# Two copies of an attention stage moved from GpSimd to ScalarE, and more dummy matmuls in front of and inside it

## The chip, the cores and the metric

The kernel runs on one core of one Trainium2 chip. The metric is the device time of one execution in microseconds (us); smaller is better. A core has TensorE (PE, with its weight loads PEld), VectorE (DVE), ScalarE (ACT), GpSimd (POOL) and SyncE (SP), each with an instruction queue of its own, and DMA queues that move data between HBM and the on-chip memory (SBUF). TensorE writes to PSUM.

## What is computed

```
S = 576; gamma = 1 - 2**(-5 - head)
ret = (q @ k.T / 8) * where(i >= j, gamma**(i - j), 0)     # 4 batches, 8 heads, 576 x 64
x = ret @ v                                                # as 2304 tokens x 512
h = x @ w_in ; x = (h * sigmoid(1.702 h)) @ w_out          # 512 -> 2048 -> 512, float64 weights
e = argmax of cosine(x, expert_emb) / tau ; gate = softmax at e
out = gate * (relu(x @ w1[e]) @ w2[e])                     # 8 experts, 512 -> 1024 -> 512
```

## The kernel before

The kernel has three stages: attention (retention), a dense layer over six blocks of 384 tokens, and the experts. All times below are counted from the start of the profiled span. Attention fills the span up to 79 us, and only there does the change act.

**Attention.** A pair `bp` is two heads of one batch; there are 16 pairs, 0 to 15. One pair has four chunks of 128 positions (`ch` 0 to 3) and a tail of 64 (`ch` 4). A *step* is one (bp, ch). The order of steps is written out by hand: pairs of even and odd number take turns. It begins (0,0), (0,1), (0,2), (1,0), (0,3), (1,1), (0,4), (1,2), and from there it repeats for every pair as (b,0), (b-1,3), (b,1), (b-1,4), (b,2), so step (b,0) comes three steps ahead of (b-1,4). At step i the program issues, in this order:

- if ch is 0: `prep(bp + 2)`, the preparation of the pair after next;
- `scores(i + 2)`: eight matmuls (L275, or four at L278 for a tail) into one of three PSUM tiles, and one masking multiply on DVE (L280);
- `state(bp, ch)`: four matmuls (L302) that add to the running state in PSUM, and one scaled copy of it to SBUF on ACT (L304), tile `ends`. The next chunk of the same pair reads that copy in L318, and the next L302 may overwrite the PSUM state only when the copy has read it;
- `chunk(bp, ch)`: L318 (earlier state times queries) and L322 (masked scores times values);
- `keep`: at ch 3 and ch 4 a DVE multiply (L340, L337). For the pairs of batches 0 and 1, after ch 4 come casts on ACT (L350), a copy on ACT (L353) and subtractions on POOL (L351).

`prep(bp)` copies the two heads' queries into a zero-padded tile `qz` (two copies of 64x512, L287, POOL), multiplies the keys by decays in place (L290, POOL; DVE for pair 0), and copies the tails' queries (two copies of 64x64, L293, POOL). Pair 0's queries come by DMA. There are four `qz` tiles (NQ = 4).

A pair's data is one DMA of 1 MB (`row`, L232) into one of five buffers. Rows 1 to 4 are asked for at the start. Row bp + 5 is asked for at the end of pair bp, on SP's queue, and goes out when matmuls no longer read the buffer. The same queue carries the decay tables, the tails (L243) and, from 24.95 us on, the dense layer's weights (`wd`, L120).

**Dummies.** At the start PE runs 34 matmuls on a tile of ones (`warm`, L251); nothing reads their result.

**Beside it.** From step 37 on the conversion of the float64 weights is dealt out in small portions between attention steps: an ACT magnitude (L150), DVE integer work (L163, L165, L170, L177), an ACT cast (L153) and a DVE subtraction (L157), about two of sixteen units before attention ends.

Of the kernel before, what the change touches and what calls it, by code (L numbers as in the profile page):

```python
# [10 lines left out]
F32 = mybir.dt.float32  # L11
# [6 lines left out]
P = 128  # L18
B, H, S, HD = 4, 8, 576, 64
NPAIR = H // 2  # L20
NCH = 4
TAIL = S - NCH * P
# [14 lines left out]
ROW = D + 2  # L37
BIG = 100000.0
LAG = 2
WARM = 34  # L40
HOLD = NF1 - LAG - 1 - KD
STOP = 1000.0
WD_AT = (7, 11, 14)
# [1 line left out]
NBUF, NQ = 5, 4  # L45
# [4 lines left out]
AK, AV, AQ, AW = NCH * P, 2 * NCH * P, 3 * NCH * P, 4 * NCH * P  # L50
TQ, TV, TAW = TAIL, 2 * TAIL, 3 * TAIL
# [11 lines left out]
def retention_moe_kernel(  # L63
# [18 lines left out]
    PE, ACT, DVE, POOL, SP = nc.tensor, nc.scalar, nc.vector, nc.gpsimd, nc.sync  # L82
# [8 lines left out]
    ones = pool.tile([P, P], BF16, name="ones")  # L91
# [35 lines left out]
    def load_due():  # L127

        if st.get("loaded"):
            while due:  # L130
                load_wd(due.pop(0))
# [71 lines left out]
    def slot(name):  # L203
        st["slots"] = st.get("slots", -1) + 1
        assert st["slots"] < HELD
        return unit_tile(name, [P, 2048], F32, st["slots"])
# [6 lines left out]
    def attention_(psum):  # L213


        row = [slot(f"row{i}") for i in range(1, NBUF)]
        row.insert(0, slot("row0"))
        qz = [slot(f"qz{i}") if i > 1 else pool.tile([P, 2048], F32, tag="tab", bufs=2, name=f"qz{i}") for i in range(NQ)]
        tb = slot("tb")[:, : NPAIR * TW].rearrange("p (n w) -> p n w", w=TW)
        ends = slot("ends")  # L220
        tl = [ends[:, NPAIR * TAW * i : NPAIR * TAW * (i + 1)].rearrange("p (n w) -> p n w", w=TAW) for i in range(2)]
# [24 lines left out]
        DVE.memset(ones, 1.0)  # L246
        ACT.copy(scr, ones[:, :16])

        warm = psum.tile([P, 512], F32, tag="o", bufs=2, name="warm")
        for _ in range(WARM):  # L250
            PE.matmul(warm[:, :P], ones, ones, start=True, stop=True)  # L251
        scs = [psum.tile([P, 512], F32, name=f"sc{i}") for i in range(3)]
        for i in range(NQ):
            for j in range(2):
# [8 lines left out]
        def scores(n):  # L263
            bp, ch = steps[n]
            t, q = row[bp % NBUF], [qz[bp % NQ][:, S * j + P * ch : S * (j + 1)] for j in range(2)]
            sc = scs[n % 3][:, : 2 * P].rearrange("p (j q) -> p j q", j=2)
            pr = pool.tile([P, 2, P], F32, tag="g", bufs=6, name=f"pr{bp}_{ch}")
            st["pr", bp, ch] = pr
            w = P if ch < NCH else TAIL
            if ch < NCH:  # L270


                for j, i in ((0, 0), (0, 1), (1, 1), (1, 0)):
                    k0, q0 = P * ch + 64 * (i ^ j), 64 * (i ^ j)
                    PE.matmul(sc[64 * i : 64 * i + 64, j, q0:], t[:, k0 : k0 + 64], q[j][:, q0:P], start=True, stop=True)  # L275
            else:
                for j in range(2):
                    PE.matmul(sc[64 * j : 64 * j + 64, j, :TAIL], tl[bp // NPAIR % 2][:, bp % NPAIR, :TQ], q[j], start=True, stop=True)  # L278
            mask = tb[:, bp % NPAIR, :TD].rearrange("p (j q) -> p j q", j=2)
            DVE.tensor_tensor(pr[:, :, :w], sc[:, :, :w], mask[:, :, :w], ALU.mult)  # L280

        def prep(bp):
            t, end = row[bp % NBUF], tl[bp // NPAIR % 2][:, bp % NPAIR, TQ:TV]
            for j in range(2):
                r, q0 = slice(64 * j, 64 * j + 64), S * j
                if bp:
                    POOL.tensor_copy(qz[bp % NQ][r, q0 : q0 + NCH * P], t[r, AQ:])  # L287
            kd = t[:, AK:AV].rearrange("p (c e) -> p c e", e=HD)
            dec = tb[:, bp % NPAIR, TD + P : TD + P + 2 * NCH]
            (POOL if bp else DVE).tensor_tensor(kd, kd, dec.unsqueeze(2).to_broadcast(kd.shape), ALU.mult)  # L290
            for j in range(2):
                r, q0 = slice(64 * j, 64 * j + 64), S * j + NCH * P
                POOL.tensor_copy(qz[bp % NQ][r, q0 : q0 + TAIL], end[r])  # L293

        def state(bp, ch):
            t = row[bp % NBUF]
            if ch == 0:
                st["kv", bp] = psum.tile([P, 64], F32, tag="kv", bufs=2, name=f"s{bp}")
            s = st["kv", bp]
            for j in range(2):  # L300
                c0 = P * ch + 64 * j
                PE.matmul(s[64 * j : 64 * j + 64], t[:, AK + c0 : AK + c0 + 64], t[:, AV + c0 : AV + c0 + 64], start=ch == 0, stop=True, skip_group_check=ch > 0)  # L302
            dec = TD + P + 2 * NCH + ch
            ACT.activation(kvs[bp % 2][:, 64 * ch : 64 * ch + 64], s, AF.Copy, scale=tb[:, bp % NPAIR, dec : dec + 1])  # L304

        def chunk(bp, ch):
            t = row[bp % NBUF]
            pr = st.pop(("pr", bp, ch))
            if ch == 0:
                st["o", bp] = psum.tile([P, 512], F32, tag="o", bufs=2, name=f"ao{bp}")  # L310
            if ch == NCH:
                st["ot", bp] = psum.tile([P, 512], F32, tag="ot", bufs=1, name=f"at{bp}")
            n = P if ch < NCH else TAIL
            o = st["o", bp][:, P * ch : P * (ch + 1)] if ch < NCH else st["ot", bp][:, :TAIL]
            if ch:
                for j in range(2):
                    q0 = S * j + P * ch
                    PE.matmul(o[64 * j : 64 * j + 64], kvs[bp % 2][:, 64 * (ch - 1) : 64 * ch], qz[bp % NQ][:, q0 : q0 + n], start=True, stop=False)  # L318
            for j in range(2):
                v0 = AV + P * ch + 64 * j  # L320
                v = t[:, v0 : v0 + 64] if ch < NCH else tl[bp // NPAIR % 2][:, bp % NPAIR, TV:]
                PE.matmul(o[64 * j : 64 * j + 64], v, pr[:, j, :n], start=ch == 0, stop=True)  # L322
# [39 lines left out]
        prep(1)  # L362
        scores(0)
        scores(1)
        for i, (bp, ch) in enumerate(steps):
            if ch == 0 and bp + 2 < NBP:
                prep(bp + 2)
            if i + 2 < len(steps):
                scores(i + 2)
            if ch < NCH:  # L370
                state(bp, ch)
            chunk(bp, ch)
            if ch >= NCH - 1:
                keep(bp, ch == NCH)
            if ch == NCH:
                if bp + NBUF < NBP:
                    load(bp + NBUF)
                if bp + NBUF in WD_AT:
                    load_wd(WD_AT.index(bp + NBUF))
                if bp + NBUF + 1 == NBP:  # L380

                    st["loaded"] = True
                    SP.dma_start(c[:, :CET], cst[:, :CET])
                    SP.dma_start(c[:, CET : CET + KD * E], embt)
                    uf = pool.tile([P, P], F32, tag="cvb", bufs=1, name="uf")
                    SP.dma_start(uf, cst[:, CU:CSL])
                    load_due()
            yield
# [325 lines left out]
    psum = ctx.enter_context(tc.tile_pool(name="psum", bufs=1, space=bass.MemoryType.PSUM, reuse_waits="tile"))  # L714
# [300 lines left out]
```

## Time and profile before

| | |
|---|---|
| device time, median of 3 runs | 785.65 us (784.45 to 787.34) |
| profiled execution, its own time | 788.28 us |
| its span | 786.4 us (1.9 us lie around it) |
| PE busy | 756.7 us (96%) |
| DVE / ACT / POOL busy | 458.3 / 306.6 / 226.6 us |
| mean granted TensorE clock | 0.985 |

The profiled execution is one run; it is 2.6 us longer than the median of the unprofiled runs. [...] In rows of the timeline the first number is the start, the second the time from the first start to the last end of the merged instructions; in brackets stands the idle time before them and what ended it.

### The profile page before, as it was taken

What the parts mean: (1) busy time and instruction counts of PE and PEld (TensorE: products, weight loads), DVE (VectorE), ACT (ScalarE), POOL (GpSimd) and SP (SyncE); (2) the same over time, 40 slices, a digit from 0 to 9 for tenths busy, and PEclk for the clock granted to TensorE, in tenths of its full rate; (3) what the DMA queues carried; (4) which work ended last, traced back from release to release, by engine and by line L of the source; (5) the groups of instructions that cost most, each with busy time, mean ns of one, the idle gap of its engine ahead of it and who ended that gap; (6) DMA issues with size and microseconds to landing.
All of it is one profiled execution on the core that took longest, in us unless ns stands there. A gap on an engine that the chain in (4) does not pass through costs nothing.

```text
span 786.4 us, 13066 instructions
## 1 busy us (share of the span) xinstructions
PE 756.7 (96%) x4996; PEld 678.1 (86%) x4996; DVE 458.3 (58%) x1000; ACT 306.6 (39%) x572; POOL 226.6 (29%) x251
## 2 busy tenths in 40 slices
PE   7998999999999889999999998999999999999994
PEld 6988899999999779989989987888888888888883
DVE  4688798886368775744763886652543435444210
ACT  2453454544553232323322443434444444445221
POOL 4995000000002211210201233234544545544311
PEclk8999999999999999999999999999999999999998
DMA  9988995001200122021004234255464635545201
GB/s 346 383 339 278 400 386 199 0 1 53 108 0 1 55 68 80 1 72 51 0 1 135 81 107 132 79 178 171 157 178 131 197 134 181 180 153 176 78 31 35
DMA packets 31576, 104.95 MB, mean 133 GB/s; under 512 B 4495, under 2 KB 7439, under 8 KB 27280
## 3 DMA queue, kind: packets, MB, share of 16 engines
q1 hardware_dynamic: 27984, 93.78, 35.1%
q0 software_dynamic: 3232, 9.46, 3.3%
q8 instruction: 41, 0.67, 0.3%
q10 hardware_dynamic: 288, 0.79, 0.3%
q14 instruction: 31, 0.25, 0.1%
HBM read 80.88 MB, written 24.18 MB: 134 GB/s over the span
## 4 chain that ended last, share of the span: by engine, by line
PE 73%; DVE 10%; issue 8%; ACT 4%; DMA 3%; POOL 2%; SPq 0%; POOLq 0%; ACTq 0%; DVEq 0%
PE h L416 20%; PE o L427 20%; PE eo L427 12%; PE eh L416 12%; DVE dj L514 4%; PE sc L275 2%; PE ao L322 2%; PE ao L318 1%; DMA row<-att 1%; PE tp L619 1%; DMA we<-we 1%; PE s L302 1%; DVE unit L195 1%; POOL out L457 1%; POOL unit L196 1%
## 5 line engine op out<-in xcount | busy, mean ns | idle before, releaser
L416 PE MATMUL h<-x,unit 128*128 128x384 f32 x1152 | 219.9, 339 | 4.7 <-DVE x_k L445 2.5
L416 PEld LDWEIGHTS h<-x,unit 128*128 128x128 f32 x1152 | 205.8, 189 | 15.1 <-DVE x_k L445 3.8
L196 POOL TENSOR_TENSOR unit<-we,unit 128x512 fp32r<-128x512 f32 x64 | 105.0, 1647 | 149.7 <-ACT unit L194 149.6
L416 PE MATMUL eh<-xt,unit 128*128 128x352 f32 x672 | 117.1, 323 | 0.0
L416 PEld LDWEIGHTS eh<-xt,unit 128*128 128x128 f32 x672 | 111.0, 188 | 6.3
L514 DVE CUSTOM_DVE_ANT_0 dj<-xr,en 128x512 f32<-128x512 f32 x120 | 91.2, 813 | 0.0
L195 DVE TENSOR_TENSOR unit<-we,unit 128x512 fp32r<-128x512 f32 x64 | 58.3, 911 | 41.0 <-ACT unit L194 41.0
L194 ACT CAST unit<-we 128x1024 fp32r<-128x1024 f32 x64 | 66.8, 1046 | 7.0 <-DMA we<-we 7.0
L480 POOL TENSOR_TENSOR enrm<-scr,c 128x8 f32<-128x8 f32 x1 | 1.7, 1683 | 150.4 <-ACT ej L485 150.4
L275 PE MATMUL sc<-qz,row 128*64 128x128 f32 (+1 forms) x512 | 38.1, 252 | 5.9 <-POOL qz L287 2.4
L280 DVE TENSOR_TENSOR pr<-sc,tb 128x256 f32<-128x256 f32 (+1 forms) x80 | 30.4, 391 | 13.3 <-PE sc L275 10.3
L457 POOL DMA_INDIRECT out<-y,idx x24 | 23.6, 981 | 49.2 <-ACT y L628 47.1
L275 PEld LDWEIGHTS sc<-qz,row 128*64 128x64 f32 x512 | 29.9, 140 | 7.9 <-POOL qz L287 3.5
L304 ACT ACTIVATE ends<-s,tb 128x64 f32<-128x64 f32 x64 | 19.7, 312 | 33.0 <-PE s L302 30.5
L322 PE MATMUL ao<-pr,row 128*64 128x128 f32 x256 | 30.0, 281 | 1.1 <-DVE pr L280 1.0
L457 POOL DMA_INDIRECT xs<-xr,slot x18 | 18.7, 1040 | 35.4 <-DVE ov_all L593 23.3
L409 POOL TENSOR_TENSOR x<-x0s,x 128x768 fp32r<-128x768 f32 x3 | 6.0, 1997 | 72.6 <-ACT x L408 72.6
L302 PE MATMUL s<-row 128*64 128x64 f32 x256 | 23.3, 228 | 0.6 <-ACT ends L304 0.4
L318 PE MATMUL ao<-qz,ends 128*64 128x128 f32 x192 | 22.7, 280 | 0.0
L157 DVE TENSOR_TENSOR unit<-ca,unit 128x1024 fp32r<-128x1024 f32 x16 | 20.4, 1276 | 2.8 <-ACT unit L153 2.8
L572 POOL TENSOR_TENSOR cum<-cum,oh_all 128x8 bf16<-128x8 bf16 x18 | 3.6, 202 | 62.4 <-PE rk L565 61.5
L322 PEld LDWEIGHTS ao<-pr,row 128*64 128x64 f32 x256 | 19.6, 141 | 2.3 <-DVE pr L280 2.1
(1258 smaller groups left out, 1545.2 us busy)
## 6 DMA issues: line engine op xcount, KB each, us to landing
we<-we SPq DMA_DIRECT2D x64, 512.0 KB, 3.5
wd<-wd SPq DMA_DIRECT2D x16, 1024.0 KB, 9.9
row<-att SPq DMA_DIRECT2D x15, 1024.0 KB, 7.1
xs<-fill SPq DMA_DIRECT2D x22, 257.0 KB, 10.4
xrow<-xr SPq DMA_DIRECT2D x18, 257.0 KB, 4.8
rin<-xs SPq DMA_DIRECT2D x8, 514.0 KB, 4.6
x0d<-x0f SPq DMA_DIRECT2D x4, 768.0 KB, 10.5
x0s<-x0d SPq DMA_DIRECT2D x8, 384.0 KB, 6.4
```

Source lines behind the costliest of these rows:

```text
L194: ACT.copy(w[:, 0, :], t)
L195: DVE.tensor_tensor(w[:, 1, :512], t[:, :512], w[:, 0, :512].bitcast(F32), ALU.subtract)
L196: POOL.tensor_tensor(w[:, 1, 512:], t[:, 512:], w[:, 0, 512:].bitcast(F32), ALU.subtract)
L275: PE.matmul(sc[64 * i : 64 * i + 64, j, q0:], t[:, k0 : k0 + 64], q[j][:, q0:P], start=True, stop=True)
L280: DVE.tensor_tensor(pr[:, :, :w], sc[:, :, :w], mask[:, :, :w], ALU.mult)
L302: PE.matmul(s[64 * j : 64 * j + 64], t[:, AK + c0 : AK + c0 + 64], t[:, AV + c0 : AV + c0 + 64], start=ch == 0, stop=True, skip_group_chec ...
L318: PE.matmul(o[64 * j : 64 * j + 64], kvs[bp % 2][:, 64 * (ch - 1) : 64 * ch], qz[bp % NQ][:, q0 : q0 + n], start=True, stop=False)
L322: PE.matmul(o[64 * j : 64 * j + 64], v, pr[:, j, :n], start=ch == 0, stop=True)
L416: PE.matmul(h, w[:, a, P * dc : P * (dc + 1)], xt[:, b, dc, :n], start=k == 0, stop=k == len(terms) - 1)
L427: PE.matmul(o, a[:, c0 : c0 + n], w[:, b, 512:], start=first and k == 0, stop=last and k == 2)
L457: i = POOL.indirect_dma_start(out=dst[:, :], out_offset=bass.IndirectOffsetOnAxis(ap=rows, axis=0), in_=src, in_offset=None, bounds_check= ...
L514: DVE.tensor_tensor_reduce(junk, r[:, :D], en[e // 4][:, e % 4, :], 1.0, 0.0, ALU.mult, ALU.add, dots[:, E * k + e : E * k + e + 1])
```

## The change

Four edits, all in attention: the number of dummies in front goes from 34 to 62, and their PSUM tile from tag `o` to tag `ot`; 8 more dummies are issued after `scores(1)` and after the chunk of each of the first three steps; the second head's query copy of pairs 4 to 15 goes from POOL to ACT; the tails' query copies of all pairs go from POOL to ACT, and from `prep(bp)` (two pairs ahead) to the point behind `chunk(bp, 1)`.

```diff
-WARM = 34
+WARM = 62
...
-        warm = psum.tile([P, 512], F32, tag="o", bufs=2, name="warm")
-        for _ in range(WARM):
-            PE.matmul(warm[:, :P], ones, ones, start=True, stop=True)
+        warm = psum.tile([P, 512], F32, tag="ot", bufs=1, name="warm")
+        def run(n):
+            for _ in range(n):
+                PE.matmul(warm[:, :P], ones, ones, start=True, stop=True)
+        run(WARM)
...
         def prep(bp):
-            t, end = row[bp % NBUF], tl[bp // NPAIR % 2][:, bp % NPAIR, TQ:TV]
+            t = row[bp % NBUF]
             for j in range(2):
                 r, q0 = slice(64 * j, 64 * j + 64), S * j
                 if bp:
-                    POOL.tensor_copy(qz[bp % NQ][r, q0 : q0 + NCH * P], t[r, AQ:])
+                    copy = ACT.copy if j and bp >= NQ else POOL.tensor_copy
+                    copy(qz[bp % NQ][r, q0 : q0 + NCH * P], t[r, AQ:])
             kd = t[:, AK:AV].rearrange("p (c e) -> p c e", e=HD)
             dec = tb[:, bp % NPAIR, TD + P : TD + P + 2 * NCH]
             (POOL if bp else DVE).tensor_tensor(kd, kd, dec..., ALU.mult)
+        def prep_tail(bp):
+            end = tl[bp // NPAIR % 2][:, bp % NPAIR, TQ:TV]
             for j in range(2):
                 r, q0 = slice(64 * j, 64 * j + 64), S * j + NCH * P
-                POOL.tensor_copy(qz[bp % NQ][r, q0 : q0 + TAIL], end[r])
+                ACT.copy(qz[bp % NQ][r, q0 : q0 + TAIL], end[r])
...
         scores(0)
         scores(1)
+        run(8)
         for i, (bp, ch) in enumerate(steps):
...
             chunk(bp, ch)
+            if i < 3:
+                run(8)
+            if ch == 1:
+                prep_tail(bp)
             if ch >= NCH - 1:
                 keep(bp, ch == NCH)
```

## Rows read from the trace of the kernel before

**Rows 1.** Windows of 5 us: PE, PEld, DVE, ACT, POOL busy, clock, DMA share, GB/s.
```profile
10.00:15.00 5.00, 3.16 (x35) 2.79 (x37) 0.47 (x2) 0.32 (x1) 3.48 (x7) 0.50 1.03 427
20.00:25.00 5.00, 5.00 (x124) 5.00 (x122) 3.76 (x10) 2.56 (x8) 4.72 (x9) 1.00 0.97 383
...
60.00:65.00 5.00, 3.85 (x88) 3.49 (x85) 4.84 (x10) 1.09 (x4) 4.66 (x7) 1.00 0.95 341
...
95.00:100.00 5.00, 5.00 (x27) 4.51 (x26) 3.58 (x6) 2.65 (x4) 0.00 (x0) 1.00 1.04 329
```
**Rows 2.** Windows of 1 us, the same columns: the clock falls and rises.
```profile
8.00:9.00 1.00, 0.81 (x15) 0.53 (x11) 1.00 (x3) 0.00 (x0) 0.23 (x1) 0.83 1.01 429
9.00:10.00 1.00, 0.65 (x6) 0.25 (x4) 0.56 (x2) 0.31 (x1) 0.24 (x1) 0.50 0.91 378
...
15.00:16.00 1.00, 1.00 (x22) 1.00 (x20) 0.38 (x1) 0.32 (x1) 0.92 (x2) 0.75 0.95 394
```
**Rows 3.** Timeline of PE, first 16 us.
```profile
1.05 3.81 PE L251 MATMUL warm<-ones 128*128 128x128 bf16 x34 [1.05 <-DVE ones L246]
5.51 0.40 PE L275 MATMUL sc<-qz,row 128*64 128x128 f32 x4 [0.65 <-DMA qz<-att]
7.33 1.10 PE L275 MATMUL sc<-qz,row 128*64 128x128 f32 x20 [1.41 <-DMA qz<-att]
8.62 0.48 PE L302 MATMUL s<-row 128*64 128x64 f32 x4 [0.19 <-DVE row L290]
...
11.84 1.35 PE L275 MATMUL sc<-qz,row 128*64 128x128 f32 x8 [2.19 <-POOL qz L287]
...
13.84 1.05 PE L275 MATMUL sc<-qz,row 128*64 128x128 f32 x8
...
15.53 0.60 PE L275 MATMUL sc<-qz,row 128*64 128x128 f32 x8
```
**Rows 4.** Groups of instructions, 0 to 140 us: the copies and their neighbours.
```profile
L287 POOL COPY qz<-row 64x512 f32<-64x512 f32 x30 | 20.1, 669 | 4.2 <-DMA row<-att 3.1
L304 ACT ACTIVATE ends<-s,tb 128x64 f32<-128x64 f32 x64 | 19.7, 312 | 33.0 <-PE s L302 30.5 <-ACT ends L304 0.9
...
L293 POOL COPY qz<-ends 64x64 f32<-64x64 f32 x32 | 9.4, 293 | 7.7 <-DMA ends<-tails 6.8
...
L353 ACT COPY x0f<-x 128x384 f32<-128x384 f32 x4 | 2.0, 512 | 4.1 <-DVE x L337 4.1
```
**Rows 5.** Timeline of ACT, 19 to 24 us: around step (2,0).
```profile
19.26 0.31 ACT L304 ACTIVATE ends<-s,tb 128x64 f32<-128x64 f32 x1
20.02 0.72 ACT L304 ACTIVATE ends<-s,tb 128x64 f32<-128x64 f32 x2 [0.45 <-ACT ends L304]
```
**Rows 6.** Timeline of PE, 19.2 to 21.2 us: L302 of step (2,1).
```profile
20.89 0.33 PE L302 MATMUL s<-row 128*64 128x64 f32 x3
```
**Rows 7.** Timeline of SP: issue of row 4, of row 8.
```profile
7.83 0.44 SPq L232 DMA_DIRECT2D row<-att  x1
...
28.26 0.33 SPq L232 DMA_DIRECT2D row<-att  x1
```
**Rows 8.** DMA issues, 7.8 to 8.6 us (row 4): us to landing last.
```profile
row<-att SPq DMA_DIRECT2D x1, 1024.0 KB, 13.0
```
**Rows 9.** DMA issues, 28 to 29 us (row 8).
```profile
row<-att SPq DMA_DIRECT2D x1, 1024.0 KB, 7.4
```
**Rows 10.** Rows 5 to 15, issued 16 to 60 us: the tile's landing line.
```profile
DMA to landing us min/median/max: 5.7/6.4/7.4
```
**Rows 11.** Timeline of ACT, 33 to 38 us: around step (6,0).
```profile
34.32 0.31 ACT L304 ACTIVATE ends<-s,tb 128x64 f32<-128x64 f32 x1
34.92 0.77 ACT L304 ACTIVATE ends<-s,tb 128x64 f32<-128x64 f32 x2 [0.30 <-PE s L302]
```
**Rows 12.** Timeline of PE, 28 to 82 us: tails of pairs 4 to 6, L302 of (6,1).
```profile
32.99 0.32 PE L318 MATMUL at<-qz,ends 128*64 128x64 f32 x3
...
35.79 0.32 PE L302 MATMUL s<-row 128*64 128x64 f32 x3
...
37.45 0.32 PE L318 MATMUL at<-qz,ends 128*64 128x64 f32 x3
...
41.13 0.32 PE L318 MATMUL at<-qz,ends 128*64 128x64 f32 x3
```
**Rows 13.** The chain that ended last, 31 to 80 us: start, us, what.
```profile
35.42 0.58 POOL x L351
36.00 0.56 POOL qz L287
36.61 0.62 POOL qz L287
...
61.47 1.15 issue
```
**Rows 14.** Timeline of all engines, 66.5 to 70 us.
```profile
67.17 2.09 DVE L157 TENSOR_TENSOR unit<-ca,unit 128x1024 fp32r<-128x1024 f32 x1
...
68.13 1.52 POOL L293 COPY qz<-ends 64x64 f32<-64x64 f32 x2
```
**Rows 15.** Line L157, its sixteen instructions: duration in ns, min/median/max.
```profile
L157 DVE TENSOR_TENSOR unit<-ca,unit x16: 1217/1221/2092, 67.2 to 191.1; 128x1024 fp32r<-128x1024 f32 x16
```
**Rows 16.** Timeline of all engines, 48 to 51 us.
```profile
48.84 1.20 ACT L150 ACTIVATE ca<-wd 128x1024 f32<-128x1024 f32 x1 [0.62 <-DMA wd<-wd]
49.94 0.50 ACT L304 ACTIVATE ends<-s,tb 128x64 f32<-128x64 f32 x2
...
50.29 0.34 PE L318 MATMUL at<-qz,ends 128*64 128x64 f32 x4 [0.23 <-ACT ends L304]
```
**Rows 17.** Timeline of PE, 76 to 88 us: the dense layer begins.
```profile
79.27 4.78 PE L416 MATMUL h<-x,unit 128*128 128x384 f32 x26 [0.31 <-DVE x0f L340]
85.06 2.03 PE L416 MATMUL h<-x,unit 128*128 128x384 f32 x10 [1.01 <-DVE unit L157]
```

## The prediction

> **What bounds the kernel now.** I read the table of 5 us windows first [rows 1]. From 85 us on PE is busy without a gap; attention, up to 79 us, has gaps, so what the change can give or take lies there. In the window from 20 us PE issues 124 instructions and is full; in the one from 60 us it issues 88. POOL is busy 4.7 of 5 us in both, so it has no reserve. The DMA share is near 1.0 all along: rows come no faster than the engines deliver them. The dense layer starts when the last attention multiply is done, waits once for a converted unit, and then runs on [rows 17]; the conversion is dealt out by steps, not by time, so that wait moves with the end of attention. I therefore take a shift of attention's end as a shift of the kernel's end, one for one.
>
> In the start PE waits three times: 0.65 and 1.41 us for pair 0's queries, and 2.19 us for pair 1's, which POOL can copy only when their DMA has landed [rows 3]. [...]
>
> **What it costs, part by part.**
>
> *Dummies in front.* 34 take 3.81 us, 0.112 us each. Another 28 take between 1.5 us (0.055, the pace of the 20 matmuls in 1.10 us at 7.33) and 3.1 us [rows 3]. They end between 6.4 and 8.0 us. The first scores, now at 5.51, slip behind them, and at worst those of 7.33 by 0.7 us. Everything PE does before 9.7 us has the 2.19 us wait in front of 11.84 behind it, so this costs nothing, and neither do the 8 dummies behind the scores and the 8 behind step 0 (0.45 to 0.9 us each set): 0.7 + 0.9 us of it push the work of step 0, still within 2.19. Without that wait they would cost their length.
>
> *Dummies behind steps 1 and 2.* These 16 do lie on PE's path: 0.9 us at the higher clock, 1.8 us at the lower. [...] The next paragraph says why I put down neither.
>
> *Query copies on ACT.* Twelve copies of 64x512. ACT copied 384 columns in 0.512 us and took 0.312 for 64 columns with a per-partition scale [rows 4]; 512 columns come to about 0.62 us. POOL sheds 12 x 0.669 = 8.0 us. ACT has the time: it is busy 2.56 of 5 us in a full window [rows 1]. But the copy stands in ACT's queue ahead of the state copy L304 of step (bp-2, 0), and it must wait for row bp to land. POOL was late with these copies, so it never showed how late rows are. Row 4, the first that moves, is asked for at 7.83 and lands 13.0 us later, at 20.8 [rows 7, 8]. ACT comes to the copy at 19.57, when L304 of step (1,2) ends, and starts L304 of (2,0) at 20.02 [rows 5]. With the copy at 20.85 to 21.47, that L304 runs from about 21.4 to 21.72. PE's L302 of step (2,1), at 20.89 now [rows 6], needs it and goes at 21.76: **+0.87 us**. Row 4's landing hangs on a DMA queue full from the start, so if the clock brings PE here 0.7 us earlier, it waits 0.7 us longer; if PE is 1.8 us late, the row has landed and only those 1.8 count. Hence zero for the clock in the sum, and 0.9 more as its upper bound.
>
> [...]
>
> Rows 5 to 15 take 5.7 to 7.4 us from issue to landing, 6.4 in the middle [rows 10]. Row 8 is one of the slow ones: issued at 28.26, 7.4 us, so at 35.7 [rows 7, 9]; ACT is there at 34.63, and 6.37 us after the issue is thus all the row may take, plus the slack of L304. Both issue and arrival move by the 0.87. The copy then runs from 36.6 to 37.2, L304 of (6,0) ends at 37.45, and L302 of (6,1), due at 35.79 + 0.87 [rows 11, 12], comes 0.8 us late: **+0.8** (0, if the row takes the middle time). The others I put at nothing, their middle latency being inside that time and slack.
>
> *What POOL gives back.* Pair 5 takes 37.45 - 32.99 = 4.46 us from tail to tail, the next 41.13 - 37.45 = 3.68 [rows 12]. The chain names POOL there: the subtraction L351, then both copies L287, done just before PE's scores [rows 13]. With less on POOL this goes: **-0.78**, at the place where row 8 now stalls. At 67.17 DVE's L157 takes 2.09 us, where the sixteen have a median of 1.22, with POOL's tail copies, 1.52 us for two, beside it [rows 14, 15]. The masked scores of two steps stand behind it. With the tails on ACT I take **-0.7** of the 0.87 (0 if another POOL instruction is in the way).
>
> [...]
>
> *Tails on ACT.* 32 copies of 64x64, at most 0.312 us each by L304's row, about 10 us over the stage, under steps in which ACT idles; POOL sheds 9.4 us [rows 4]. Behind the conversion's ACT work (1.20 us for an L150 [rows 16]) an added copy may delay a state copy: **+0.2** (0 to 1.2 for two full collisions). The move itself, to behind chunk 1, leaves several steps before the tail's scores, and costs nothing.
>
> The sum: 0.87 + 0.8 - 0.78 - 0.7 + 0.2 = +0.4 us. The profiled execution would go from 788.28 to 788.7; the median of the runs shown is 2.6 us under it, so I say 786.0.
>
> **Rivals.**
> - *Relief pays* (0.20). The state copies keep enough slack and rows come a little sooner: no stall on rows, the clock's 0.7 kept, POOL's 0.78 and DVE's 0.87 back, and the 1.15 us in the chain at 61.47 that nothing visible explains [rows 13] gone with POOL's backlog: -3.5 us, 782.1. For it: POOL is full all the way. Against: row 4 lands 1.2 us after ACT asks, whatever PE does.
> - *Every row blocks ACT* (0.12): the slower side. Place: ACT's copy in step (bp-2, 0). If all rows took 7.4 us, each would stop the state copies for 7.4 - 6.37 - 0.35 = 0.7 us or, at PE's full pace, where issue and arrival lie closer, 0.9; over 11 rows 7.7 to 10, with 0.87 for row 4 and 1.3 back from POOL and DVE +7 to +9.5 us: 793 to 795. It decides (slower by over 3.9 us) from 0.4 us a row, a mean latency of about 7.1 us. Against: 6.4 in the middle now.
> - *The clock falls all the same* (0.15): the change does not do that part. [...]
>
> **How the numbers follow.** About 0.5%, 3.9 us, is what a measurement of this kernel can tell from no change. The forecast, 786.0, has 0.53. Its own range is 784 to 788 by the bounds above: -1.5 if both row stalls are 0 (-1.3) with the contention's last 0.17; +2 with the clock's 0.9 and the collisions' 1.2 together. To hold 8 in 10 it reaches to most of the relief case and the clock case: 782.7 to 788.7. Under 781.7 lies about half of the relief case and little else: 0.12. Above 789.6 lie most of the blocking case: 0.10. Between: 0.78.
>
> **What would show it.** In the changed profile: a wait of PE's L302 for L304 near 21 us, with ACT idle until row 4 lands at 20.8; the same or nothing near 36 us; POOL with gaps in every 5 us window from 25 us on; no PE wait for the copies L287 after pair 2; DVE's L157 at 1.2 us; a clock of 1.00 or 0.50 between 12 and 15 us without a change of what PE does after 22 us. I am wrong if ACT reaches the copies later than its state copies suggest, if rows land sooner than now, or if ACT waits for rows in the second half too.

## The result

The changed kernel takes 789.04 us (median of 9 runs, 787.34 to 794.02); beside it on the same chip the kernel before takes 785.42 us (9 runs, 784.45 to 787.34). The ratio is 1.0057, 95% interval 1.0040 to 1.0075: slower by some 3.6 us and above the predicted range. The profiled execution of the changed kernel took 788.17 us with a span of 786.4 us, and before's took 788.28 us with the same span. So the two traces look level although the kernels are not; where the execution of before lost its time is shown below.

### The profile after

**The start.** Windows of 1 us, columns as in [rows 2], then the timeline of PE:

```profile
11.00:12.00 1.00, 0.04 (x2) 0.04 (x2) 0.00 (x0) 0.00 (x0) 0.64 (x2) 1.00 1.06 439
12.00:13.00 1.00, 0.84 (x9) 0.53 (x11) 0.00 (x0) 0.00 (x0) 0.91 (x2) 0.59 0.91 363
13.00:14.00 1.00, 1.00 (x16) 0.98 (x12) 0.42 (x1) 0.43 (x2) 0.71 (x1) 0.50 1.07 437
...
15.00:16.00 1.00, 1.00 (x18) 0.80 (x17) 0.00 (x0) 0.00 (x0) 0.92 (x2) 0.70 0.92 381
```
```profile
1.05 5.67 PE L254 MATMUL warm<-ones 128*128 128x128 bf16 x62 [1.05 <-DVE ones L246]
...
9.51 0.62 PE L254 MATMUL warm<-ones 128*128 128x128 bf16 x8
11.96 0.51 PE L280 MATMUL sc<-qz,row 128*64 128x128 f32 x4 [1.83 <-POOL qz L293]
...
14.32 1.03 PE L254 MATMUL warm<-ones 128*128 128x128 bf16 x8
...
16.46 0.62 PE L254 MATMUL warm<-ones 128*128 128x128 bf16 x8
...
19.62 0.29 PE L327 MATMUL at<-qz,ends 128*64 128x64 f32 x4
```

In this execution the dummies put off the fall of the clock from the ninth microsecond to the thirteenth and do not prevent it: PE still idles for 1.83 us in front of 11.96, and the clock is back in the sixteenth as in [rows 2]. The 8 dummies at 14.32 run at a granted clock of 0.50 and take 1.03 us; those at 16.46 follow at 1.00 and take 0.62. Pair 0's tail starts at 19.62, in before at 18.09: +1.53 us. That is one execution; another of the same order of work, shown with the experiments, keeps its clock.

**Rows awaited on ACT.** Timeline of all engines near steps (4,0) and (6,0), in two extracts:

```profile
29.83 0.61 ACT L293 COPY qz<-row 64x512 f32<-64x512 f32 x1 [1.46 <-DMA row<-att]
...
30.47 0.52 ACT L313 ACTIVATE ends<-s,tb 128x64 f32<-128x64 f32 x2
...
30.84 0.34 PE L311 MATMUL s<-row 128*64 128x64 f32 x4 [0.88 <-ACT ends L313]
```
```profile
38.04 0.61 ACT L293 COPY qz<-row 64x512 f32<-64x512 f32 x1 [1.04 <-DMA row<-att]
...
39.05 0.34 PE L311 MATMUL s<-row 128*64 128x64 f32 x4 [0.62 <-ACT ends L313]
```

This is the predicted stall: ACT stands at the copy until the row lands (1.46 and 1.04 us), the state copy comes behind it, and PE waits for that (0.88 and 0.62 us). In this execution it is at rows 6 and 8, not at 4 and 8; PE came to row 4 1.5 us later than in before, and by then the row was there.

**The relief.** Groups of instructions of the first 140 us as in [rows 4], and two of the 5 us windows as in [rows 1]:

```profile
L293 POOL COPY qz<-row 64x512 f32<-64x512 f32 x18 | 10.9, 607 | 25.7 <-DMA row<-att 13.7 <-PE sc L283 4.9 <-PE at L331 2.5
L302 ACT COPY qz<-ends 64x64 f32<-64x64 f32 x32 | 7.6, 236 | 0.4
L293 ACT COPY qz<-row 64x512 f32<-64x512 f32 x12 | 7.4, 616 | 4.1 <-DMA row<-att 3.5 <-issue 0.3
```
```profile
20.00:25.00 5.00, 5.00 (x126) 5.00 (x122) 3.55 (x11) 4.07 (x13) 4.31 (x6) 1.00 0.83 291
...
60.00:65.00 5.00, 4.66 (x111) 4.42 (x109) 4.91 (x11) 2.42 (x9) 1.61 (x2) 1.00 0.96 349
```

POOL is down from 4.66 to 1.61 us in the window from 60 us, and PE issues 111 instructions there instead of 88.

**The seam to the dense layer.** Timeline of PE, the rows that answer [rows 17]:

```profile
81.66 4.78 PE L430 MATMUL h<-x,unit 128*128 128x384 f32 x26 [1.04 <-DVE x0f L346]
...
87.45 1.83 PE L430 MATMUL h<-x,unit 128*128 128x384 f32 x9 [1.01 <-DVE unit L157]
```

The last tail, first after, then before:

```profile
80.17 0.34 PE L327 MATMUL at<-qz,ends 128*64 128x64 f32 x4
```
```profile
78.51 0.34 PE L318 MATMUL at<-qz,ends 128*64 128x64 f32 x4
```

Dense starts 81.66 - 79.27 = 2.39 us later. But the last tail starts at 80.17, in before at 78.51, which is only 1.66 later. The other 0.73 us lie in the wait: 1.04 for L346, the multiply of the last tail, where before waited 0.31 us for L340, the multiply of the last whole chunk.

**The end.** The last scatter on POOL and the semaphore instructions of the branch line behind it (duration in ns min/median/max, first and last start), first after, then before:

```profile
775.40 0.92 POOL L471 DMA_INDIRECT out<-y,idx  x1 [1.09 <-ACT y L642]
```
```profile
L663 POOLq EVENT_SEMAPHORE  x5: 17/42/43, 778.5 to 780.9; - x5
```
```profile
777.30 0.92 POOL L457 DMA_INDIRECT out<-y,idx  x1 [1.09 <-ACT y L628]
```
```profile
L649 POOLq EVENT_SEMAPHORE  x5: 17/43/43, 780.6 to 780.9; - x5
```

Each of the five takes at most 43 ns. In before they start within 0.3 us; in the changed kernel they are spread over 2.4 us. From the end of the scatter to the end of the span before takes 786.41 - 778.22 = 8.19 us, the changed kernel 786.38 - 776.32 = 10.06 (10.07 with the trace's nanoseconds). The DMA packets that bring instructions, on queue q14, in that stretch, first after, then before (count, MB, share):

```profile
q14 instruction: 4, 0.03, 1.1%
```
```profile
q14 instruction: 3, 0.02, 1.0%
```

The changed kernel has one such packet of 8 KB more.

**Between.** From the first dense matmul to the end of the last scatter the same work takes 698.96 us in before and 694.65 in after. Windows of 6 us, first before, then after:

```profile
258.00:264.00 6.00, 3.91 (x17) 3.08 (x16) 4.81 (x14) 1.49 (x3) 0.64 (x3) 0.77 0.00 0
...
294.00:300.00 6.00, 6.00 (x21) 5.37 (x20) 2.29 (x10) 1.59 (x4) 3.01 (x3) 0.60 0.73 263
```
```profile
258.00:264.00 6.00, 4.00 (x25) 3.48 (x24) 5.42 (x17) 1.77 (x5) 0.45 (x2) 1.00 0.00 0
...
294.00:300.00 6.00, 6.00 (x33) 5.58 (x32) 4.12 (x19) 2.00 (x6) 3.37 (x5) 1.00 0.66 241
```

Before's profiled execution had a granted clock of 0.50 for a while at two places, near 261 and near 292 us, and PE issued 21 instructions in place of 33 in the last of these windows. The changed kernel's execution had neither. The table below the experiments shows that such falls come and go with the execution, in versions of every kind. So the stage's 4.31 us are no gain of the change; by estimate, without them before's execution would have taken 788.28 - 4.31, about 784 us.

The account between these two executions is thus: dense starts 2.39 us later (1.53 the start, 0.13 the rest of attention, 0.73 the seam), the stage is 4.31 shorter by the clock, the end 1.88 longer. The seam and the end return in other executions as they are here; the start and the rest of attention do not.

### The profile page after: what moved, and what is told of

It reads as the page before. It is cut to its first block, busy times and chain, and to the rows that moved or that the text cites. A ratio compares the mean times of both kernels' runs of the same rounds, so it can differ in the third digit from the quotient of the medians.

```text
span 786.4 us, 13171 instructions
## 1 busy us (share of the span) xinstructions
PE 756.0 (96%) x5056; PEld 677.2 (86%) x5056; DVE 458.0 (58%) x1000; ACT 320.1 (41%) x616; POOL 207.6 (26%) x207
## 4 chain that ended last, share of the span: by engine, by line
PE 69%; DVE 11%; issue 9%; ACT 4%; DMA 4%; POOL 2%; SPq 0%; POOLq 0%; ACTq 0%; DVEq 0%
PE h L430 20%; PE o L441 20%; PE eo L441 12%; PE eh L430 11%; DVE dj L528 4%; DMA row<-att 2%; PE sc L280 2%; PE ao L331 1%; POOL unit L196 1%; PE tp L633 1%; DMA we<-we 1%; DVE unit L195 1%; PE ao L327 1%; POOL out L471 1%; DVE h L454 1%
## 5 line engine op out<-in xcount | busy, mean ns | idle before, releaser
L280 PE MATMUL sc<-qz,row 128*64 128x128 f32 (+1 forms) x512 | 33.5, 250 | 2.3 <-POOL qz L293 2.0
L331 PE MATMUL ao<-pr,row 128*64 128x128 f32 x256 | 25.8, 278 | 1.3 <-DVE pr L285 0.9
L311 PE MATMUL s<-row 128*64 128x64 f32 x256 | 19.3, 227 | 2.4 <-ACT ends L313 2.4
L157 DVE TENSOR_TENSOR unit<-ca,unit 128x1024 fp32r<-128x1024 f32 x16 | 19.8, 1237 | 2.8 <-ACT unit L153 2.8
L170 DVE SCALAR_TENSOR_TENSOR ca<-wd,ca 128x1024 int32<-128x1024 int32 x16 | 20.4, 1274 | 0.3
L177 DVE SCALAR_TENSOR_TENSOR ca<-wd,ca 128x1024 int32<-128x1024 int32 x16 | 19.5, 1217 | 0.0
```

What stands on the lines that cost most here:

```text
L157: DVE.tensor_tensor(units[u][:, 1, :], word(u).bitcast(F32), units[u][:, 0, :].bitcast(F32), ALU.subtract)
L170: DVE.scalar_tensor_tensor(a, d[:, :, 1], -0x40000000, a, ALU.bitwise_and, ALU.bitwise_or)
```

## The experiments

Theory: the loss is made of things that the prediction had at nothing, the dummies behind steps 1 and 2 and a later end of the program. Rivals: ScalarE's own added load and its waits for rows are the loss; or the loss lies in the dense stage. Every ratio is against the kernel before, run on the same chip; "falls" are stretches at a granted clock of 0.50 between 250 and 300 us, named by where they begin.

**One half each.** The copies on ScalarE alone (the dummies as before, 34 and none behind, but in tag `ot`), and the dummies alone.

```diff
-WARM = 62
+WARM = 34
...
-        run(8)
...
-            if i < 3:
-                run(8)
```


> The changed kernel without any of the added dummies (34 in front, none behind): the moves to ScalarE alone. Theory (two separate losses, dummies +1.5 us and rows that hold up ScalarE about +2 us, against some 2 us of relief late in attention): the first steps are as in the kernel before, TensorE waits for the state copies where rows land late (row 4 near 21 us, one or two of rows 6 to 8), and the median is +0.5 to +2 us over the kernel before, 786 to 787.5. Rival (the dummies are the whole loss, ScalarE's copies are free): 784 to 785.4, no wait for state copies over 0.3 us before 42 us. Second rival (the copies are the whole loss): 788.5 or more.

The dummies alone, against the changed kernel; the tails' copies also go back into `prep`:

```diff
-                    copy = ACT.copy if j and bp >= NQ else POOL.tensor_copy
-                    copy(qz[bp % NQ][r, q0 : q0 + NCH * P], t[r, AQ:])
+                    POOL.tensor_copy(qz[bp % NQ][r, q0 : q0 + NCH * P], t[r, AQ:])
...
-                ACT.copy(qz[bp % NQ][r, q0 : q0 + TAIL], end[r])
+                POOL.tensor_copy(qz[bp % NQ][r, q0 : q0 + TAIL], end[r])
```


> The kernel before with all the added dummies, and no copy moved. Theory: the clock falls about 3.4 us later than before, just when the row of pair 1 has landed, and rises where it rose; the 16 dummies behind steps 1 and 2 cost 1.5 us by the tail of pair 0 (19.6 us in place of 18.1). GpSimd is the pacer from there to about 38 us, so part of the 1.5 is absorbed and the stall of 0.78 us at pair 5 shrinks: +0.5 to +1.5 us, 786 to 787. Rival (dummies cost nothing or help, the ScalarE copies are the whole loss): within 0.5 us of 785.4.

Copies alone: 789.08 us, ratio 1.0046 (1.0031 to 1.0060). Dummies alone: 786.15, 1.0010 (0.9992 to 1.0029). The copies look like the culprit, but their trace says otherwise: dense starts at 79.75, only 0.48 later than before, and the end takes 10.07 us. Here PE is early enough for ACT to wait for row 4 (timeline of ACT):

```profile
20.87 0.61 ACT L293 COPY qz<-row 64x512 f32<-64x512 f32 x1 [0.66 <-DMA row<-att]
24.22 0.62 ACT L293 COPY qz<-row 64x512 f32<-64x512 f32 x1
29.03 0.62 ACT L293 COPY qz<-row 64x512 f32<-64x512 f32 x1 [1.15 <-DMA row<-att]
```

The row was there at 20.87; the prediction had 20.85.

In the dummies alone the forecast of the time held, but not its mechanism: the clock did not fall. Pair 0's tail starts at 18.35, where 19.6 was expected.

**Dummies only in the waits.** Before's copies, 62 dummies in front, 8 behind `scores(1)`, 40 behind step 0 and none later. The edit against the dummies alone:

```diff
-            if i < 3:
-                run(8)
+            if i < 1:
+                run(40)
```


> The kernel before with 62 dummies in front, 8 behind the first two scores and 40 behind step 0, so that TensorE is busy up to about 11.8 us, and none behind steps 1 and 2. Theory: the dummies that lie in waits are free, and the clock stays at 1.00 through 12 to 16 us; the tail of pair 0 comes 1.3 to 1.6 us earlier than 18.09, and GpSimd, which is full from 18 us on, takes most of it back by the tail of pair 5: -0.3 to -1.5 us. Rival (the clock falls whatever fills the wait): no gain, the tail of pair 0 at 18.1 or later, +0 to +0.5 us.

786.69 us, 1.0013 (0.9994 to 1.0032). The clock stays up (one window of 10 us, columns as in [rows 2]):

```profile
8.00:18.00 10.00, 9.73 (x197) 8.93 (x195) 5.19 (x13) 2.68 (x9) 5.81 (x12) 1.00 1.02 421
```

Pair 0's tail starts 1.31 us earlier than in before, but pair 4's only 0.07: on the way PE waits for POOL's copies, where before has no wait (timeline of PE):

```profile
28.30 0.43 PE L279 MATMUL sc<-qz,row 128*64 128x128 f32 x4 [0.24 <-POOL qz L291]
...
32.75 0.43 PE L279 MATMUL sc<-qz,row 128*64 128x128 f32 x4 [0.24 <-POOL qz L291]
```

POOL sets the pace there, and a won start alone is given back. The time missed its forecast of -0.3 to -1.5 us; with tag `ot` this version too carries the longer wait at the seam.

**The copy one chunk later.** ACT's query copy of pair bp goes behind chunk 2 of pair bp - 2.

```diff
-                if bp:
-                    copy = ACT.copy if j and bp >= NQ else POOL.tensor_copy
-                    copy(qz[bp % NQ][r, q0 : q0 + NCH * P], t[r, AQ:])
+                if bp and not (j and bp >= NQ):
+                    POOL.tensor_copy(qz[bp % NQ][r, q0 : q0 + NCH * P], t[r, AQ:])
...
+        def prep_late(bp):
+            ACT.copy(qz[bp % NQ][64:, S : S + NCH * P], row[bp % NBUF][64:, AQ:])
...
+            if ch == 2 and NQ <= bp + 2 < NBP:
+                prep_late(bp + 2)
```


> The changed kernel, with ScalarE's query copy of pair bp issued four steps later (behind chunk 2 of pair bp - 2), when its row has landed. Theory (rows hold up ScalarE): the waits of TensorE for state copies near 31, 39 and 47 us go, and the median is 1 to 2 us under the changed kernel's 789.0: 787 to 788. Rival (it is ScalarE's load that costs, not the wait for rows): within 0.5 us of 789.0, the waits only move to other steps.

788.23 us, 1.0038 (1.0019 to 1.0056). None of the twelve copies waits for a row any more, but dense still starts at 81.77. The start's loss of 1.70 stays; between 16 and 80 us PE's waits for state copies go from 2.4 to 0.8 us, and its waits for DVE's masking multiplies from 0.9 to 2.1. In this execution the row waits are not what makes attention late.

**The length of POOL's instruction stream.** The versions with the long end so far have 416 POOL instructions, the others 491. So I added small memsets of an 8-column tile at POOL's start, which nothing waits for: 75 and 8 to the changed kernel, 53 to the kernel before.

```diff
-        POOL.memset(cum, 0.0)
+        for _ in range(54):
+            POOL.memset(cum, 0.0)
```


> The changed kernel with 75 tiny memsets more on GpSimd at 2 to 9 us, where it idles, so that its instruction stream is as long as in the kernel before (491 executed, 416 in the changed one). Theory (GpSimd's last block, after the last scatter, now lies across two pieces of code, and the second is fetched only when it is reached, about 2 us): the time from the last GpSimd scatter to the end of the span goes from 10.1 us back to about 8.2, and the median falls by 2 us to about 787. Rival (the late end is a wait for data or for another engine): 10 us stay, 789.

> The kernel before with 53 tiny memsets more on GpSimd at 2 to 8 us, nothing else; 491 + 53 = 544 = 416 + 128 instructions. Theory (code in pieces of 128 instructions): the last block lies as in the changed kernel, the end grows from 8.2 to about 10.1 us, and the median goes up by 2 us to about 787.1. Rival (the end depends on the moved copies, not on the length of the stream): no change, 785.1.

> The changed kernel with 8 tiny memsets more on GpSimd at its start. Theory: in the changed kernel the second piece begins two instructions into the last block, so 8 instructions push the whole block into one piece: 8.2 us from the last scatter to the end. Rival (the number of fetches goes with the length of the stream): 10 us as in the changed kernel.

The kernel before with 53 memsets: 787.77 us, 1.0027 (1.0010 to 1.0045), with attention 0.63 us shorter and an end of 10.07 us. The same five instructions as above, on its own branch line:

```profile
L650 POOLq EVENT_SEMAPHORE  x5: 17/43/43, 778.3 to 780.7; - x5
```

The changed kernel with 8, a single run: 786.28 us, an end of 8.07 us:

```profile
L664 POOLq EVENT_SEMAPHORE  x5: 17/43/43, 778.7 to 779.0; - x5
```

So the long end can be given to the kernel before and taken from the changed one by instructions that do nothing. It is not the ScalarE copies as such. The 75 memsets were mis-sized as padding: 791.48 us, 1.0081 (1.0058 to 1.0104), end 8.00 us, but POOL came late to pair 1's copies (timelines of POOL and of PE):

```profile
1.87 12.23 POOL L267 MEMSET cum<- 128x8 bf16 x76
```
```profile
14.70 1.36 PE L281 MATMUL sc<-qz,row 128*64 128x128 f32 x8 [4.59 <-POOL qz L294]
```

**Tails alone with the dummies in the waits**, padded by 40 memsets for the short end; all query copies on POOL.

```diff
-                    copy = ACT.copy if j and bp >= NQ else POOL.tensor_copy
-                    copy(qz[bp % NQ][r, q0 : q0 + NCH * P], t[r, AQ:])
+                    POOL.tensor_copy(qz[bp % NQ][r, q0 : q0 + NCH * P], t[r, AQ:])
...
-            if i < 3:
-                run(8)
+            if i < 1:
+                run(40)
```


> The kernel before with the tails' copies alone on ScalarE (behind chunk 1), the query copies all on GpSimd, dummies only where TensorE waits (62 in front, 8 behind the first two scores, 40 behind step 0), and 40 memsets on GpSimd against the late fetch. Theory (tails cost ScalarE nothing, since it never waits for a row; GpSimd has room again, so that the 1.3 us won at the start are kept): attention ends 1.5 to 2.5 us earlier than 79.27, the end is 8.2 us, 783 to 784.5. Rival (ScalarE's 32 copies cost by their number): attention ends at 79 or later, 785 or more.

784.35 us, 0.9985 (0.9971 to 0.9998): the only version whose interval lies below before. Pair 0's tail is 1.21 us earlier and the last still 0.98. That the won start is kept with less on POOL is not shown, though: in the second execution of these edits, with tag `o` below, pair 0's tail is 1.32 earlier and the last 0.07.

**The terms one at a time, with the short end.** Four versions, in this order: the changed kernel with 8 memsets; the copies alone with 8; the tails alone without any added dummies, with 40; the late copy with dummies only in the waits, with 8.

> The changed kernel with 8 small memsets on POOL in front, which only lengthen its instruction stream. If the late end is a matter of how long POOL's stream is: 8.0 to 8.2 us from the end of the last scatter to the end of the span instead of 10.07, and a median of about 787.1 us, so some 2 us of the change's 3.6 are the end and 1.5 to 2 us are attention. If the late end has to do with ScalarE's copies themselves: 10 us and 789.

> ScalarE's copies of queries and tails alone (34 dummies, none behind), with the same 8 memsets. If the dummies are worth nothing net: the same as the changed kernel with the memsets, about 787 us. If the dummies cost what attention's start lost (1.5 us at the first pair's tail): 785.5 to 786, and dense starts about 1.5 to 2 us earlier than in the changed kernel. The end 8.0 to 8.2 us.

> Tails on ScalarE, all query copies back on POOL, the dummies as before (34, none behind), padded so that the end is the short one. If the gain of the tails-only kernel with dummies in the waits (0.15%) came from the tails: the same, 784.4 us. If it came from the dummies in the waits: 785.4 to 786, level with before.

> All query copies and tails on ScalarE, each copy put one chunk later so that no row is awaited in front of an eviction, dummies only in the two long waits (62, 8, 40) and 8 memsets. If the change's loss is the sum of the row waits, of dummies outside waits and of the late end: 783 to 784.5 us, below before by 0.1 to 0.3%. If ScalarE's own load is the loss: 786 or more.

In the same order: 788.01 us, 1.0040 (1.0022 to 1.0058); 786.41, 1.0013 (1.0000 to 1.0026); 786.77, 1.0015 (0.9998 to 1.0033); 786.02, 1.0005 (0.9992 to 1.0018). The first and the fourth came out 0.9 and 1.5 us over their forecasts (the fourth just where its rival, ScalarE's own load, began) and the third over both of its alternatives, though all ends are short (8.01 to 8.05 us). In each of the four the first dense matmul waits 1.04 us, as in the changed kernel and in the dummies alone, and that led to the last question.

The first of them is the program that gave the single run above, and its profiled execution went another way. One window of 10 us, first that run, then this execution, and this execution's PE at row 4:

```profile
8.00:18.00 10.00, 8.18 (x122) 6.39 (x119) 2.96 (x7) 1.57 (x6) 4.51 (x6) 0.83 1.02 422
```
```profile
8.00:18.00 10.00, 7.94 (x147) 6.54 (x144) 3.92 (x10) 2.12 (x8) 4.51 (x6) 1.00 1.02 419
```
```profile
22.13 0.34 PE L312 MATMUL s<-row 128*64 128x64 f32 x4 [0.78 <-ACT ends L314]
```

In the one the clock fell and pair 0's tail came at 19.63; in the other it stayed up and the tail came at 18.38, but then PE waited 0.78 us for the state copy behind row 4.

**The dummies' tile back in tag `o`**, in four of these versions.

```diff
-        warm = psum.tile([P, 512], F32, tag="ot", bufs=1, name="warm")
+        warm = psum.tile([P, 512], F32, tag="o", bufs=2, name="warm")
```


> The changed kernel with 8 memsets on POOL, and the dummies' tile in tag o, as before the change. If the tag shifts the PSUM tiles: the first dense matmul waits 0.31 us for the multiply L350 (that of the last chunk) in place of 1.04 us for the tail's, dense starts 0.73 us earlier against the last tail than with tag ot, and the median is about 787.3 us or 0.7 under the changed kernel with memsets. If the dummies or copies are the cause: 1.04 us still.

> Copies of queries and tails on ScalarE alone, 34 dummies in tag o, 8 memsets. If the tag is the cause: dense 0.73 us earlier against the last tail, and 785.0 to 785.7 us, level with before: the copies themselves then neither bring nor cost anything that can be measured. If not: 786.4.

> Only the tails on ScalarE, dummies only in the two long waits, tag o, padded for the short end. If the tag is the cause: 783.3 to 783.8 us, 0.2 to 0.3% under before. If not: 784.4.

> All copies on ScalarE, query copies one chunk later, dummies only in the two long waits, tag o, 8 memsets. If the tag is the cause: 0.7 us under the same with tag ot, 784.3 to 785.3, level with before. If not: 786.

786.82 us, 1.0015 (0.9998 to 1.0031); 786.38, 1.0001 (0.9983 to 1.0019); 785.18, 0.9987 (0.9970 to 1.0003); 785.07, 0.9992 (0.9975 to 1.0008). By their ratios the second and the fourth are level with before, as the tag's forecasts said; the third missed its 0.2 to 0.3% gain. The ratios of three fall by 0.12 to 0.25% against the same with tag `ot`; that of the tails alone, 0.9985 to 0.9987, does not move. The trace decides: the wait is gone in all four. Timeline of PE, changed kernel with memsets and tag `o`:

```profile
80.22 4.78 PE L431 MATMUL h<-x,unit 128*128 128x384 f32 x26 [0.31 <-DVE x0f L350]
```

All profiled executions in one table, worked out from their traces (us; "dense" is the start of the first dense matmul with its wait, "stage" runs from there to the end of the last scatter, "end" from there to the end of the span; falls by the microsecond nearest to their beginning; times are rounded, so sums can be off by 0.01):

```
version              POOL instr.  dense (wait)   stage    end    falls
before                   491      79.27 (0.31)  698.96   8.19   261, 292 (long)
changed                  416      81.66 (1.04)  694.65  10.07   none
copies alone             416      79.75 (1.04)  697.42  10.07   263, 293
dummies alone            491      79.51 (1.04)  696.14   8.10   261
dummies in waits         491      78.81 (1.04)  697.64   8.23   261, 292
copy later               416      81.77 (1.04)  694.70  10.46   none
changed + 75             491      85.43 (1.04)  696.32   8.00   297
before + 53              544      78.64 (0.31)  697.42  10.07   261, 292
changed + 8, single run  424      80.49 (1.04)  695.94   8.07   292
tails, waits             480      79.02 (1.04)  694.18   7.93   none
changed + 8              424      81.78 (1.04)  696.72   8.05   263
copies alone + 8         424      80.13 (1.04)  694.15   8.01   none
tails alone              480      79.85 (1.04)  697.24   8.04   262, 293
late copy, waits         424      80.69 (1.04)  695.73   8.01   262
changed + 8, tag o       424      80.22 (0.31)  696.73   8.23   292
copies alone + 8, tag o  424      80.00 (0.31)  697.45   8.20   262, 293
tails, waits, tag o      480      79.20 (0.31)  697.37   8.26   262, 293
late copy, waits, tag o  424      78.62 (0.31)  696.13   8.14   260
```

The stage goes by the falls: 694.2 to 694.7 us without one, 695.7 to 696.7 with one, 697.2 to 697.6 with two, 698.96 in before's execution, whose second fall was the longest. The kernels differ in the other two columns. More falls are not what makes the changed kernel slower: in the timed runs of changed + 8 its mean granted clock is 0.991, as before's on that chip, at 1.0040 of the time. Two executions of the same program (changed + 8) have dense starts 1.3 us apart, so a dense start from one trace is good to about that much.

## Why the prediction was wrong

**The step that failed** is "I therefore take a shift of attention's end as a shift of the kernel's end, one for one." The end had a term of its own, +1.88 us, of which the sum knew nothing; without it, by estimate, 789.04 us would have been about 787, inside the range. Four comparisons measure it against the same work: 10.07 less 8.07 us in the traces of the changed kernel without and with 8 memsets; 1.0057 against 1.0040 in their timings (1.3 us) and 1.0046 against 1.0013 in the copies alone (2.6 us); 1.0027, 2.1 us, when it was given to the kernel before.

**Dummies and clock, put at zero: some 1 to 2 us.** Zero rested on row 4: whatever the start won or lost would be hidden by ACT's wait for it, with 0.9 us more as the upper bound. As far as pair 1 that was right. In the profiled execution the clock fell, pair 0's tail was 1.53 us late, the row had landed, and pair 1's tail was 1.53 late too. Where the clock stayed up, in changed + 8, pair 0's tail was 0.29 late, PE waited 0.78 for row 4, and pair 1's tail was 1.29 late. In the four executions of the changed order that still wait for rows (with and without memsets, either tag) pair 1's tail is 1.06 to 1.55 us late, in the three of the copies alone 0.89 to 1.09; the sum had 0.87. The 0.7 us at which the prediction puts the worth of the clock are its author's estimate, and no run shows them; between the two executions of changed + 8, with the clock down and up, lie 1.25 us at pair 0's tail (19.63 and 18.38). What was mis-sized is the dummies' cost at the end of attention: the last tail is on average 1.22 us later than in before in those four, 0.20 in those three. The timings give 1.0040 against 1.0013 (2.1 us), 1.0015 against 1.0001 (1.1 us) and 1.0057 against 1.0046 (0.9 us), all with the copies on ACT. With the copies on POOL the dummies alone are at 1.0010, tag included. How some 0.3 us at pair 1 become 1 us at the last pair no run shows.

The rival *the clock falls all the same* (chance 0.15) came true in half: of the six executions with 8 dummies behind step 0 and a wait of about 1.8 us after them the clock fell in three, with pair 0's tail at 19.62 to 19.79, and stayed up in three, at 18.27 to 18.38. The dummies of step 0 are done at about 10.1 us, long before pair 1's queries are copied. With 40 dummies there it stayed up in all five. With before's 34 dummies and none behind, pair 0's tail itself lies between 18.09 and 19.18 in six executions, so the 1.53 us between two traces come in part from the execution and not from the kernel.

**The tag, not priced at all: +0.73 us.** In the program the dummies' tile is the first one made in PSUM. In tag `ot` it puts the attention tails' tile where it had been the chunks' (tag `o`), and the first dense matmul, which reuses that place, waits for the last reader of the tail. This last sentence is read from the order in the code; the wait itself is shown, 1.04 us in the twelve executions with `ot`, 0.31 in the six with `o`.

**Query copies on ACT: mechanism right, place off.** Forecast +0.87 at row 4 and +0.8 at row 8. Measured in the changed kernel's profiled execution: 0 at row 4, 0.88 at row 6, 0.62 at row 8, and 0.78 at row 4 where the clock stayed up; the copy took 0.616 us where 0.62 was estimated. Both forecasts have ACT start nothing ahead of a copy that waits. So it was at rows 6 and 8: by 29.19 and 37.66 us PE had done the matmuls of the two state copies behind each, and ACT began these at 30.47 and 38.68, 0.03 us after the end of the copy that had waited for the row. From issue to the copy row 6 took 29.83 - 22.33 = 7.5 us and row 8 38.04 - 29.70 = 8.3, against the 6.4 and 7.4 I had used.

**Relief of POOL: right, and larger.** Against before, the tails win 1.05 us back at pair 11, where the chain of before held the 1.15 us that nothing explained [rows 13], and 0.92 at pair 13, where I had -0.7. There DVE's L157 takes at most 1.489 us, in before 2.092 [rows 15]; first the line after, then the instruction of before that ran beside the first microsecond of L157, ahead of the tails' copies of [rows 14]:

```profile
L157 DVE TENSOR_TENSOR unit<-ca,unit x16: 1212/1219/1489, 69.1 to 193.4; 128x1024 fp32r<-128x1024 f32 x16
```
```profile
67.14 1.04 POOL L290 TENSOR_TENSOR row<-row,tb 128x512 f32<-128x512 f32 x1
```

With POOL's copies gone from beside it 0.60 of the 0.87 us came back; the key multiply L290 (L296 after, 68.45 to 69.49 us), which the prediction did not name, still runs beside the beginning of L157 (69.08). Why L157 takes longer beside POOL's work the traces do not show; the 0.7 was an estimate from the two standing side by side. After pair 0 attention's gains and losses sum to 1.66 - 1.53 = +0.13 us in these two executions, where the terms for it gave +0.4.

**The base.** I took 788.28 us as an ordinary execution 2.6 us over the median for no known reason. Its excess goes with the clock falls of the stage, 698.96 us against some 694.4 in the executions without one.

Taking the causes out one after the other, each ratio against before on its own chip:

```
changed                            1.0057   1.0040 to 1.0075
 and the short end                 1.0040   1.0022 to 1.0058
 and tag o                         1.0015   0.9998 to 1.0031
 and before's 34 dummies           1.0001   0.9983 to 1.0019
```

The intervals of neighbours overlap, so a single step of this ladder is not proved by its times alone. The end and the tag have rows of their own in the traces (the tag's step, 2.0 us, is more than its row's 0.73); for the dummies there are the three pairs of timings, and no row. What is left at its foot, the two copies on ScalarE, is worth nothing that can be measured (-1.3 to +1.5 us by its interval). The best version kept only the tails on ScalarE and put the dummies into the waits; at -0.15% with one tag and -0.13% with the other its gain is about 1 us; the interval of the first barely leaves out no change, that of the second includes it.

Open stays what POOL does in the 2 us in the end. That the chip fetches a further piece of the program there is an inference, with two supports. One is the instruction counts: 416 and 544 have the long end, and they are 128 apart; 424, 480 and 491 have the short one. The other is the packets of q14: between the last scatter's end and the end of the span all four executions with the long end have four, all fourteen with the short end three. In the long ones a packet of 8 KB lands within POOL's gap, and POOL goes on 1.17 to 1.24 us after it; in the copy later both come 0.4 us later, which is its 10.46. But the short ones have a packet at about that time too, the additional one starts only 0.7 to 0.9 us after POOL has gone on, and no row says which engine a packet is for. The runs show a dependence on the count, and two counts 128 apart behave alike; pieces of 128 instructions, as in the expectation for the kernel before with 53 memsets, are a guess that fits the five counts, and no row shows how many instructions a piece holds. Why the clock falls in some executions and not in others, at the start and near 261 and 292 us, was not tried either.

## What to carry to other kernels

Before trusting a base, split its span into stages and compare each with the same stage of another execution: clock falls in a stage that the change does not touch hid 4.31 us here and made two unequal kernels look alike. For the same reason read the price of an edit from several executions: one trace had the start 1.53 us late, another of the same order 0.29. Price every edit at the end of the program too, since moving instructions from one queue to another changes the lengths of both (here 416 in place of 491 on POOL, with 1.88 us more at the end), and price a renamed buffer, since here it moved its neighbours and with them the wait at the next stage (1.04 us in place of 0.31). Dummies held the clock here every time they filled the wait to its end, and in three of six executions when they left 1.8 us of it; even so POOL, which set the pace, could take the time won back.

## What the hardware showed that I had not expected

- The end of the program is 7.9 to 8.3 or 10.07 us (10.46 once) behind the last scatter, by the number of POOL instructions: 8 added instructions take 2.0 us away, 53 add 1.9. POOL goes on after its gap 1.17 to 1.24 us behind the landing of a packet of the instruction queue.
- A memset of 8 columns on POOL, 104 ns by itself, costs 0.16 us in a chain (76 in 12.23 us).
- In 14 of 18 profiled executions the granted clock fell to 0.50 once or twice between 260 and 300 us, in a stage that is the same in all of them. With one such fall the stage takes 1.3 to 2.3 us more than without, with two some 3.0.
- With the same dummies in front of the same wait the clock at the start fell in three executions of six and stayed up in three; one program did both in two executions.
